# The row maxima of a second query block, moved in among the first projections of a gated two-branch attention

## Chip, core and metric

The kernel runs on one core of a Trainium2 chip. The metric is the device time of one execution in microseconds (us), over three runs the median. A difference of 0.2% is about what such a measurement can tell from none.

## What is computed

Two attention branches read the same x (2048 rows, 640 columns), each with weights of its own, 32 heads of 20 columns. A gate mixes them.

```python
def branch(x, wqkv, wo):                      # S = 2048, D = 640, H = 32, Dh = 20
    q, k, v = split_heads(x @ wqkv)           # each [H, S, Dh]
    p = softmax(q @ k.T * Dh ** -0.5)         # [H, S, S]
    return join_heads(p @ v) @ wo

g = sigmoid((x * gate_w).sum(-1, keepdims=True))
out = g * branch(x, A_wqkv, A_wo) + (1 - g) * branch(x, B_wqkv, B_wo)
```

## The kernel before

**Tiles and stages.** The 64 heads of both branches are 16 groups of four heads (`g`); two heads stand as `j` = 0, 1 in the upper and lower half of the partitions, in two `pair`s. Queries are cut into four blocks (`qb`) of 512, so there are 64 blocks, and each block's keys into eight *steps* `G` of 256: 512 steps in all (`STEPS`). In one step PE makes eight score tiles of 128 keys by 512 queries (`scores`, L639), ACT turns each into an exponential `pt` (L642), and in the next step PE multiplies these with the values into `acc` (`values`, L657).

**Row maxima.** The exponentials need each query's row maximum before they start. It is found from a second set of scores, queries by keys: `max_mm` (L565) makes a matmul (L581) for each head `j`, 128 queries (a unit `u`; eight units a block, `NS`) and 512 keys (`ch` = 0 to 3). In one way (`two`) two chunks of keys are done together: the first matmul takes the difference of the keys of two chunks (`KD`), ACT makes its relu (L585), and DVE adds the second chunk's scores and takes the largest (L589, a custom instruction with a read of its accumulator). In the other way DVE reduces one chunk directly (L592). The first block (u < 8) goes wholly in the first way; the others of group 0 only for `ch` 0 and 1. The partial maxima are in `mpart`, cleared by `max_parts` (L561) on POOL. `finish_max` (L596) reduces them (DVE), scales and splits them (POOL), and copies them on SP to a scratch `m_scr` and from there into rows of `QT` (L613, L617). Then the block is `ready`, and its score matmul yields scores less the maximum.

**Ahead of the loop.** x is turned and split into two f16 parts, and keys and queries of group 0 are projected (L937 to L943). What remains of the first projections is the generator `rest` (L951): three chunks of further query columns (`r_chunk`, 15 matmuls of 512 columns each) and 16 tiles of values (`project_v`, 15 matmuls of 161 columns each). `mms` (L375) yields after each matmul there. The loop at L959 goes over 16 *half units* of block 0: four score matmuls of maxima each (two chunks, two heads), then `go_on(BETWEEN)`, which takes products from `rest` until the planner's clock of PE has gone on by 1.3 us. Then block 0's chain (`finish_max`) is issued, and all that is left of `rest` runs at once.

**The main loop** (L1112) writes the order out by hand. A string of `STEP` (L51) lists what a step does: `e0`, `e1` a score for head 0 or 1, `m0`, `m1` a quarter of the step's maxima, `V` values, `X` a slot of projection. The maxima come from the list `maxima` (L1076), in the order of units; `next_maxima` (L1083) hands out a unit a step (eight matmuls) if the next unit is at least 14 ahead of the step, else one and a half (`RAMP`, twelve matmuls), and none if it is 15 (`LEAD`) or more ahead. At the loop's start the next unit is 8.

**Banks and queues.** Seven PSUM banks of 512 columns (`take`, `give`) hold scores, maxima and projections alike; a planner with fixed costs picks the bank that should come free first. The engines work off their own instructions in order; they wait for one another by semaphores.

Of the kernel before, what the change touches and what calls it, by code (L numbers as in the profile page):

```python
# [11 lines left out]
F32 = mybir.dt.float32  # L12
# [7 lines left out]
P = 128  # L20
# [4 lines left out]
NT = S // P  # L25
NC = D // P
# [3 lines left out]
QB = 512  # L30
NQ = S // QB
NS = 8
STEPS = 2 * NG * NQ * NS
# [19 lines left out]
        "X m0 m1 e0 m1 e0 e1 V e1 e0 m1 m0 V e1 m0 m1 m0 e0 e1 X")  # L53
LATE = "e0 e1 e0 e1 V X e0 e1 e0 e1 V"
RAMP = 1.5
BETWEEN = 1.3
NB = 7

T_SCORE, T_MODE, T_VALUES, T_READY = 0.217, 0.1, 0.85, 0.39
T_EXP, T_MAX, T_BACK = 0.478, 0.6, 0.15  # L60
REST = 6
PRODUCT = "product"
ORDER = (0, 2, 1, 3)
LOW = -3.0e38
# [4 lines left out]
def kernel(  # L69
# [10 lines left out]
    nc = tc.nc  # L80
# [42 lines left out]
    clock = {"pe": 0.0, "done": 0.0, "act": 0.0, "dve": 0.0}  # L123
    rows_free = [0.0, 0.0]
    block_end = [0.0, None]
    free_at, held = [0.0] * NB, set()
    now = [-1]

    def take():

        i = min((k for k in range(NB) if k not in held), key=lambda k: free_at[k])
        held.add(i)
        return i, banks[i]
# [16 lines left out]
    def tick_block(cost, ready=0.0):  # L150

        begin = block_end[0] if now[0] < 0 and block_end[1] == rows_free else max(rows_free) + T_MODE
        clock["pe"] = max(begin, ready)
        rows_free[:] = [clock["pe"] + cost + T_MODE] * 2
        block_end[:] = [clock["pe"] + cost, list(rows_free)]
        clock["done"] = clock["pe"] + cost + T_READY - T_MODE
# [124 lines left out]
    side = []  # L281
# [9 lines left out]
    def advance():  # L291
        for gen in list(side):
            goes = step_on(gen)
            if not goes:
                side.remove(gen)
                if goes is False:
                    parked.append(gen)
# [77 lines left out]
    def mms(i, out_ap, pairs, cost):  # L375

        if now[0] >= 0:
            tick_block(len(pairs) * cost * T_SCORE, free_at[i])
        for k, (a, b) in enumerate(pairs):
            if now[0] < 0:  # L380
                tick_block(cost * T_SCORE, free_at[i])
            nc.tensor.matmul(out_ap, a, b, start=(k == 0), stop=(k == len(pairs) - 1))  # L382
            if now[0] < 0:
                yield

    def turns(n):

# [32 lines left out]
    def run(gen):  # L420
        for _ in gen:
            pass
# [136 lines left out]
    relus, relu_at = {}, {}  # L559

    def max_parts(g, qb):  # L561
        m = mparts[g, qb] = wts.tile([P, 2, 2, 4, 4], F32, name="mpart", tag="mpart", bufs=2)
        nc.gpsimd.memset(m[:, :, 0:1 if g else 2, :, 0] if g or qb else m, LOW)

    def max_mm(u, ch, heads=(0, 1)):  # L565

        g, qb, i = unit_of(u)  # L570
        pair, t = divmod(i, 4)
        if (g, qb) not in mparts:
            max_parts(g, qb)
        q0 = qb * QB + t * P
        for j in heads:
            two = u < NS or ch < 2 and (j == 0 or g == 0)
            i, pt = take()
            ready = tick_score(j, i)
            r = slice(64 * j, 64 * j + 60)
            k = KD[g % 2 if ch == 0 else 1][r, pair] if two and ch % 2 == 0 else KT[g % 2][r, pair, ch * QB:(ch + 1) * QB]  # L580
            nc.tensor.matmul(pt, QT[g % 2][r, pair, q0:q0 + P], k, start=True, stop=True)  # L581
            m = mparts[g, qb][:, pair, j, t, ch:ch + 1]
            if two and ch % 2 == 0:
                relus[u, j] = start.tile([P, QB], F32, name="rl0", bufs=4) if u < NS else work.tile([P, QB], F32, name="rl", bufs=2)
                nc.scalar.activation(relus[u, j], pt, AF.Relu)  # L585
                back = relu_at[u, j] = spend("act", T_EXP, ready)
            elif two:
                rl = relus.pop((u, j))
                nc.vector.tensor_tensor_reduce(rl, pt, rl, 1.0, LOW, OP.add, OP.max, m)  # L589
                back = spend("dve", T_MAX, max(ready, relu_at.pop((u, j))))  # L590
            else:
                nc.vector.tensor_reduce(m, pt, axis=AX.X, op=OP.max)  # L592
                back = spend("dve", T_MAX, ready)
            give(i, back)
# [240 lines left out]
    start = start_stack.enter_context(tc.tile_pool(name="start", bufs=1))  # L835
# [44 lines left out]
            turn(j0, c)()  # L880
            yield

    max_parts(0, 0)
    load, split_next = weights_a(1)
    load()
    drains = [turn(0, c) for c in range(NC)] + [turn(4, 0)]
# [63 lines left out]
    split_next()  # L950
    rest = series(*(r_chunk(ch, (0, 1)) for ch in (1, 2, 3)), *(project_v(0, j) for j in range(0, NT, 2)))  # L951

    def go_on(us):

        end = clock["pe"] + us
        while clock["pe"] < end and next(rest, PRODUCT) is not PRODUCT:
            pass

    for half in range(2):  # L959
        for u in range(NS):  # L960
            for ch in (2 * half, 2 * half + 1):
                max_mm(u, ch, (1, 0))
            go_on(BETWEEN)
    while side:
        advance()
    chain = finish_max(0, 0)
    for _ in chain:
        go_on(0.5)
    run(rest)
    start_stack.close()  # L970

# [1 line left out]
    work = ctx.enter_context(tc.tile_pool(name="work", bufs=2))  # L973
# [99 lines left out]
        except StopIteration:  # L1073
            current.clear()

    maxima = [(u, ch) for u in range(NS, STEPS) for ch in ORDER]  # L1076
    debt = [0.0]

    def spread_of(u):
# [32 lines left out]
    for G in range(STEPS + 1):  # L1112
        g, qb, i = unit_of(G)
# [12 lines left out]
        for what in (STEP[blocks] if maxima or some else LATE + " X" * (blocks == 2)).split():  # L1126
            k = count[what] = count.get(what, 0) + 1
            if what[0] == "e":
                q = sum(count.get(f"e{j}", 0) for j in range(2)) - 1
                j = int(what[1])  # L1130
# [55 lines left out]
```

## Time and profile before

| | |
|---|---|
| median of 3 runs | 2802.12 us (2801.08 to 2802.19) |
| profiled execution, its own time | 2800.33 us |
| its span | 2798.5 us |
| mean granted clock of PE | 0.995 |
| busy: PE, ACT, DVE, POOL | 98%, 90%, 88%, 24% |

Times in the trace count from the start of the span. The half units begin at 57.6 us, the first projection of the main loop at 95.24 us, its first exponential at 97.36 us. A row of the timeline gives start, length, engine, line, operation, output <- input, and in brackets how long the engine had waited and for what. A row of the view by stretches gives the stretch, its length, then for PE, its weight loads (PEld), DVE, ACT and POOL the busy time and the number of instructions, and last PE's granted clock, the share of the DMA engines and GB/s; asked for one line alone, it has that line's engine only. A row of groups gives busy time and mean ns of one behind the bar, and then the idle time ahead of it. A matmul's length is modelled, and consecutive ones overlap.

### The profile page before, as it was taken

The page shows a single profiled execution, that of the slowest core. Times are in us where ns is not written, and L with a number is a line of the kernel's source. Part 1 is how long each engine was busy: PE and PEld are TensorE (multiplying, and loading weights), DVE is VectorE, ACT ScalarE, POOL GpSimd, SP SyncE. Part 2 cuts the span into 40 slices and gives each one's busy share as a digit, 9 for nine tenths or more (in the row PEclk, how much of TensorE's full clock was granted, in tenths as well). Part 3 has the DMA queues.
Part 4 walks back from the last instruction along what each step waited for, and adds up shares of the span by engine and source line. Part 5 has one row for each costly group of instructions (what it writes and reads, how often), then busy time and mean ns, then how long its engine had stood idle before and what let it go on. Part 6 is the DMA issues. An engine that isn't in the chain of part 4 may idle for free.

```text
span 2798.5 us, 61863 instructions
## 1 busy us (share of the span) xinstructions
PE 2744.9 (98%) x23122; PEld 939.9 (34%) x23122; DVE 2452.3 (88%) x4795; ACT 2524.6 (90%) x5106; POOL 671.9 (24%) x914
## 2 busy tenths in 40 slices
PE   6999999999999999999999999999999999999998
PEld 3433332333333332333333323333333333322222
DVE  6789899889999999888888988989988898999982
ACT  3799999999999999999999889999999999989987
POOL 5322122312222421321221212222342202200111
PEclk9999999999999999999999999999999999999999
DMA  4020102001020211202012231122201112131112
GB/s 136 19 57 14 41 11 46 7 21 25 14 64 17 62 27 54 48 8 61 21 35 70 58 77 31 38 63 54 61 23 42 33 46 63 31 88 55 42 48 75
DMA packets 172943, 124.57 MB, mean 45 GB/s; under 512 B 103264, under 2 KB 142488, under 8 KB 172640
## 3 DMA queue, kind: packets, MB, share of 16 engines
q1 hardware_dynamic: 170096, 118.99, 16.9%
q8 instruction: 181, 2.97, 0.4%
q0 software_dynamic: 1600, 0.96, 0.2%
q14 instruction: 122, 1.00, 0.1%
q10 hardware_dynamic: 944, 0.66, 0.1%
HBM read 54.54 MB, written 31.85 MB: 31 GB/s over the span
## 4 chain that ended last, share of the span: by engine, by line
PE 92%; DVE 3%; ACT 2%; DMA 1%; POOL 1%; issue 1%; SPq 0%; POOLq 0%; ACTq 0%; DVEq 0%
PE acc L657 35%; PE bank L581 19%; PE bank L382 19%; PE bank L639 18%; DVE mpart L592 2%; ACT pt L642 1%; DMA xs<-in_A_x_dram 0%; ACT rl L585 0%; DMA wv<-in_A_wqkv_dram 0%; PE bank L820 0%; DVE rl L589 0%; PE bank L190 0%; SPq L428 0%; DVE ot L743 0%; PE bank L869 0%
## 5 line engine op out<-in xcount | busy, mean ns | idle before, releaser
L642 ACT ACTIVATE pt<-bank 128x512 f32<-128x512 f32 x4096 | 2169.2, 612 | 166.7 <-PE bank L639 101.7
L592 DVE TENSOR_REDUCE mpart<-bank 128x1 f32<-128x512 f32 x2976 | 1865.2, 682 | 222.2 <-PE bank L581 114.8
L657 PE MATMUL acc<-pt,v 128*21 128x512 f32 x8192 | 1082.2, 600 | 0.6 <-DVE ot L743 0.4
L639 PE MATMUL bank<-qt,kt 64*128 64x512 f16 x4096 | 1051.7, 380 | 4.2 <-ACT pt L642 2.0
L581 PE MATMUL bank<-kt,qt 60*128 60x512 f16 x3536 | 1021.3, 380 | 5.1 <-ACT pt L642 1.7
L581 PEld LDWEIGHTS <-qt 60*128 60x128 f16 x4096 | 238.1, 94 | 862.9 <-issue 802.9
L589 DVE CUSTOM_DVE_ANT_0 rl<-bank,rl 128x512 f32<-128x512 f32 x560 | 378.7, 680 | 16.7 <-ACT rl L585 10.6
L585 ACT ACTIVATE rl<-bank 128x512 f32<-128x512 f32 x560 | 329.7, 595 | 10.7 <-PE bank L581 8.7
L639 PEld LDWEIGHTS <-kt 64*128 64x128 f16 x4096 | 235.5, 94 | 238.7 <-issue 122.8
L382 PE MATMUL bank<-xx,wbh 128*128 128x168 f16 (+3 forms) x2400 | 286.0, 239 | 2.6 <-ACT xx L873 1.9
L657 PEld LDWEIGHTS acc<-pt,v 128*21 128x21 f32 x8192 | 143.1, 99 | 428.8 <-issue 421.9
L382 PE MATMUL bank<-xx,wbl 128*128 128x168 f16 (+3 forms) x1200 | 256.1, 237 | 0.0
L751 POOL TENSOR_TENSOR ot<-ot,sq 128x512 f32<-128x512 f32 x63 | 66.0, 1047 | 773.4 <-DVE sq L748 773.4
L382 PEld LDWEIGHTS <-wbh 128*128 128x128 f16 x2400 | 189.4, 98 | 109.5 <-issue 102.0
L581 PE MATMUL bank<-kd,qt 60*128 60x512 f16 x560 | 203.8, 380 | 1.6 <-DMA kd<-dd 1.2
L382 PE MATMUL bank<-woh,o_in 128*128 128x320 f16 (+1 forms) x640 | 156.4, 302 | 5.5 <-DMA o_in<-o_scr 5.4
L411 POOL CAST cq<-fs 128x512 f16<-128x512 f32 x60 | 36.6, 610 | 521.0 <-ACT fs L409 517.4
L382 PE MATMUL bank<-wvh,xx 128*128 128x160 f16 (+1 forms) x1280 | 155.2, 234 | 0.1
L382 PEld LDWEIGHTS <-xx 128*128 128x128 f16 x1920 | 131.5, 97 | 52.3 <-issue 49.1
L382 PE MATMUL bank<-wvl,xx 128*128 128x160 f16 (+1 forms) x640 | 137.3, 231 | 0.5 <-POOL wvl L322 0.5
L382 PEld LDWEIGHTS <-wbl 128*128 128x128 f16 x1200 | 117.4, 98 | 4.3 <-issue 0.8
L382 PEld LDWEIGHTS <-o_in 128*128 128x128 f16 (+1 forms) x960 | 80.9, 97 | 97.7 <-issue 63.8
(131 smaller groups left out, 1259.1 us busy)
## 6 DMA issues: line engine op xcount, KB each, us to landing
y_scr<-y_out SPq DMA_DIRECT2D x48, 320.0 KB
y_out<-y_scr SPq DMA_DIRECT2D x32, 320.0 KB
kt<-cq SPq DMA_DIRECT2D x120, 80.0 KB
o_scr<-on SPq DMA_DIRECT2D x240, 40.0 KB
o_in<-o_scr SPq DMA_DIRECT2D x64, 96.0 KB
kt<-cq SPq DMA_DIRECT2D x136, 40.0 KB
wstage<-in_B_wqkv_dram SPq DMA_DIRECT2D x13, 400.0 KB
xs<-in_A_x_dram SPq DMA_DIRECT2D x8, 640.0 KB
```

Source lines behind the costliest of these rows:

```text
L382: nc.tensor.matmul(out_ap, a, b, start=(k == 0), stop=(k == len(pairs) - 1))
L411: nc.gpsimd.tensor_copy(hi, f)
L581: nc.tensor.matmul(pt, QT[g % 2][r, pair, q0:q0 + P], k, start=True, stop=True)
L585: nc.scalar.activation(relus[u, j], pt, AF.Relu)
L589: nc.vector.tensor_tensor_reduce(rl, pt, rl, 1.0, LOW, OP.add, OP.max, m)
L592: nc.vector.tensor_reduce(m, pt, axis=AX.X, op=OP.max)
L639: nc.tensor.matmul(et, KT[g % 2][r, pair, kt * P:(kt + 1) * P], QT[g % 2][r, pair, qb * QB:(qb + 1) * QB], start=True, stop=True)
L642: nc.scalar.activation(pt, et, AF.Exp, scale=factor(g // 4))
L657: nc.tensor.matmul(acc[32 * h:32 * h + VW, :], V[(g // 2) % 2][:, kt, (g % 2) * GH + h, :], ptiles.pop((G, kk, h)), start=(kt == 0), stop= ...
L751: nc.gpsimd.tensor_tensor(t3, t3, sq.unsqueeze(2).to_broadcast([P, 16, 32]), op=OP.mult)
```

## The change

Block 1's maxima (u = 8 to 15) are made ahead of the main loop too. There are 32 half units then, and `rest` is spread over them by count of its matmuls' columns (`streamed`, `whole`) instead of by the planner's clock: after each half unit 1/32 of it, after the last all. Block 0's chain is issued after the 16th half unit, block 1's after the last. All eight units of block 1 go by relu and difference for all four chunks. Both blocks' partial maxima are cleared at the start, whole. The main loop's list begins with unit 16, its rules are the same.

```diff
-BETWEEN = 1.3
+AHEAD = 2
...
+    streamed = [0.0]
...
                 tick_block(cost * T_SCORE, free_at[i])
+                streamed[0] += cost * T_SCORE
...
-                yield
+                yield True
...
-        nc.gpsimd.memset(m[:, :, 0:1 if g else 2, :, 0] if g or qb else m, LOW)
+        nc.gpsimd.memset(m[:, :, 0:1 if g else 2, :, 0] if g or qb >= AHEAD else m, LOW)
...
-            two = u < NS or ch < 2 and (j == 0 or g == 0)
+            two = u < AHEAD * NS or ch < 2 and (j == 0 or g == 0)
...
-    max_parts(0, 0)
+    for qb in range(AHEAD):
+        max_parts(0, qb)
...
-    def go_on(us):
+    halves_done = [0]
+    streamed[0] = 0.0
+    whole = (3 * 3 * NC + NT * 3 * NC * 0.33) * T_SCORE
+
+    def go_on(share):
...
-        end = clock["pe"] + us
-        while clock["pe"] < end and next(rest, PRODUCT) is not PRODUCT:
+        while streamed[0] < share * whole and next(rest, None) is not None:
             pass
...
-    for half in range(2):
-        for u in range(NS):
-            for ch in (2 * half, 2 * half + 1):
-                max_mm(u, ch, (1, 0))
-            go_on(BETWEEN)
-    while side:
-        advance()
-    chain = finish_max(0, 0)
-    for _ in chain:
-        go_on(0.5)
+    for block in range(AHEAD):
+        for half in range(2):
+            for u in range(block * NS, (block + 1) * NS):
+                for ch in (2 * half, 2 * half + 1):
+                    max_mm(u, ch, (1, 0))
+                halves_done[0] += 1
+                go_on(halves_done[0] / (2 * AHEAD * NS))
+        while side:
+            advance()
+        run(finish_max(0, block))
     run(rest)
...
-    maxima = [(u, ch) for u in range(NS, STEPS) for ch in ORDER]
+    maxima = [(u, ch) for u in range(AHEAD * NS, STEPS) for ch in ORDER]
```

On ACT, at the end of the part ahead of the loop, before: `rl` is a relu for maxima, two of them make a half unit, and `v` with `gates` drains a tile of values.

```order
L585 ACTIVATE rl_856<-bank_94 128x512
L585 ACTIVATE rl_859<-bank_89 128x512
L537 ACTIVATE v_86<-bank_92 128x8x20
L542 ACTIVATE gates<-bank_92,inv_g 128x1
L537 ACTIVATE v_86<-bank_93 128x8x20
L542 ACTIVATE gates<-bank_93,inv_g 128x1
L537 ACTIVATE v_86<-bank_91 128x8x20
L542 ACTIVATE gates<-bank_91,inv_g 128x1
```

The same place on ACT in the changed kernel:

```order
L587 ACTIVATE rl_1080<-bank_90 128x512
L587 ACTIVATE rl_1083<-bank_94 128x512
L587 ACTIVATE rl_1101<-bank_92 128x512
L587 ACTIVATE rl_1104<-bank_95 128x512
L539 ACTIVATE v_86<-bank_91 128x8x20
L544 ACTIVATE gates<-bank_91,inv_g 128x1
L587 ACTIVATE rl_1125<-bank_89 128x512
L587 ACTIVATE rl_1128<-bank_92 128x512
```

Before, nine tiles of values are drained one after the other behind the last relus; in the changed kernel relus go on to the end, with a tile of values behind each pair or each second pair.

On ACT at the start of the main loop, before: `fs` drains a projection, `pt` is an exponential, `rl` a relu for block 1's maxima.

```order
L409 ACTIVATE fs<-bank_91 128x176
L628 TENSOR_LOAD esc_103
L642 ACTIVATE pt<-bank_94 128x512
L585 ACTIVATE rl<-bank_89 128x512
L585 ACTIVATE rl<-bank_95 128x512
L642 ACTIVATE pt<-bank_92 128x512
L642 ACTIVATE pt<-bank_90 128x512
L642 ACTIVATE pt<-bank_95 128x512
L642 ACTIVATE pt<-bank_93 128x512
L642 ACTIVATE pt<-bank_90 128x512
L585 ACTIVATE rl<-bank_91 128x512
```

The same place on ACT in the changed kernel:

```order
L411 ACTIVATE fs<-bank_90 128x176
L630 TENSOR_LOAD esc_103
L644 ACTIVATE pt<-bank_93 128x512
L644 ACTIVATE pt<-bank_91 128x512
L644 ACTIVATE pt<-bank_94 128x512
L644 ACTIVATE pt<-bank_89 128x512
L644 ACTIVATE pt<-bank_95 128x512
L644 ACTIVATE pt<-bank_92 128x512
L644 ACTIVATE pt<-bank_90 128x512
L644 ACTIVATE pt<-bank_93 128x512
L411 ACTIVATE fs<-bank_91 128x168
```

The relus are gone from steps 0 and 1; in step 2 they are back, two a step.

On SP, behind the copies of group 0's queries, before: `m_scr` and `qt<-m_scr` are a block's chain, `wstage` the weights of the next values, `kd` and `kt` the keys of group 1.

```order
L613 DMA m_scr_123<-m4r 16x4x32 x4
L617 DMA qt_80<-m_scr_123 4x512 x4
L240 DMA wstage<-in_A_wqkv_dram 128x5x160
L428 DMA kd_85<-dd 40x1x512
L430 DMA kd_85<-dd 20x512
L613 DMA m_scr_124<-m4r 16x4x32 x4
```

The same place on SP in the changed kernel:

```order
L615 DMA m_scr_123<-m4r 16x4x32 x4
L619 DMA qt_80<-m_scr_123 4x512 x4
L615 DMA m_scr_124<-m4r 16x4x32 x4
L619 DMA qt_80<-m_scr_124 4x512 x4
L241 DMA wstage<-in_A_wqkv_dram 128x5x160
L430 DMA kd_85<-dd 40x1x512
```

Block 1's chain stood among the copies of group 1's keys and now stands ahead of the weights for the next values.

More of the change, by code (lines that the diff above doesn't have):

```diff
@@ L583, in max_mm @@
             if two and ch % 2 == 0:
[L584 removed]
+                relus[u, j] = start.tile([P, QB], F32, name="rl0", bufs=4) if u < AHEAD * NS else work.tile([P, QB], F32, name="rl", bufs=2)
                 nc.scalar.activation(relus[u, j], pt, AF.Relu)
```

## The prediction

> **What bounds the kernel now.** I read the page first: the busy times, then the chain that ended last.
>
> ```profile
> span 2798.5 us, 61863 instructions
> PE 2744.9 (98%) x23122; PEld 939.9 (34%) x23122; DVE 2452.3 (88%) x4795; ACT 2524.6 (90%) x5106; POOL 671.9 (24%) x914
> PE 92%; DVE 3%; ACT 2%; DMA 1%; POOL 1%; issue 1%; SPq 0%; POOLq 0%; ACTq 0%; DVEq 0%
> ```
>
> TensorE (PE) is busy for 98% of the span and carries 92% of the chain. No later idle time can swallow what is won or lost at the front, so the sum can be made at the front alone. The program order says how far the front goes: apart from the numbers of PSUM banks, every engine's instructions stand in the old order again from about step 17 of the 512 steps of the main loop.
>
> Next I cut the front of the main loop into stretches of eight steps. One step has eight exponentials (L642), so 64 of them mark a stretch; the second view gives all engines in the same stretches, and in steps 15 to 17 alone (24 exponentials).
>
> ```profile
> 97.30:152.80 55.50, 34.35 (x64) 0.97 0.08 18
> 152.80:200.10 47.30, 34.11 (x64) 1.00 0.31 72
> 283.10:324.50 41.40, 33.97 (x64) 1.00 0.29 61
> ```
> ```profile
> 97.30:152.80 55.50, 52.64 (x397) 19.34 (x394) 47.47 (x114) 47.42 (x96) 14.34 (x16) 0.97 0.08 18
> 152.80:200.10 47.30, 46.39 (x394) 16.66 (x393) 41.09 (x88) 43.87 (x92) 11.84 (x17) 1.00 0.31 72
> 195.20:210.75 15.55, 15.46 (x143) 5.36 (x140) 13.60 (x30) 15.28 (x33) 1.10 (x2) 1.00 0.22 59
> ```
>
> The first eight steps take 55.5 us, the next eight 47.3, ordinary ones 41.4. In the order of before, steps 0 to 9 carry 12 score matmuls for maxima each (eight are the even rate), since the lead of the maxima is still being built up. In the first stretch PE, ScalarE (ACT) and VectorE (DVE) all have idle time (52.6, 47.4 and 47.5 of 55.5): it isn't one full engine but twelve maxima fighting eight exponentials for seven banks. In steps 15 to 17, with the even rate and two relus a step, ACT is busy for 15.28 of 15.55 us.
>
> Ahead of the loop lie the first projections with block 0's maxima among them (the stretch from 57.60), and from 86.15 a tail of products alone.
>
> ```profile
> 57.60:95.24 37.64, 37.07 (x348) 22.46 (x349) 24.23 (x78) 25.23 (x67) 28.22 (x45) 1.00 0.20 44
> 86.15:95.24 9.09, 9.09 (x130) 9.06 (x129) 1.90 (x8) 4.55 (x18) 0.89 (x4) 1.00 0.03 4
> ```
>
> PE is full there (37.07 of 37.64), ACT (25.23) and DVE (24.23) are not. So a maximum that is moved ahead pays full PE time there, and frees the loop of work that three engines contend for.
>
> **The change part by part.** *(a) 16 more half units ahead of the loop.* A half unit is four score matmuls of maxima and the products behind it. These are PE's rows for two, with six products of 512 columns between, and the first score matmuls of two more, with 15 value products between:
>
> ```profile
> 59.67 0.39 PE L581 MATMUL bank<-kd,qt 60*128 60x512 f16 x2
> 60.20 1.04 PE L382 MATMUL bank<-xx,wbh 128*128 128x512 f16 x4
> 61.08 0.59 PE L382 MATMUL bank<-xx,wbl 128*128 128x512 f16 x2
> 61.60 0.39 PE L581 MATMUL bank<-kd,qt 60*128 60x512 f16 x2
> 64.08 1.47 PE L382 MATMUL bank<-xx,wbh 128*128 128x512 f16 x6
> 82.24 0.39 PE L581 MATMUL bank<-kd,qt 60*128 60x512 f16 x2
> 83.94 0.39 PE L581 MATMUL bank<-kd,qt 60*128 60x512 f16 x2
> ```
>
> Six products cost six times (1.47 − 0.38)/5 = 0.218 us, or 1.31; a half unit without its products is 61.60 − 59.67 − 1.31 = 0.62 us. From the value products: 83.94 − 82.24 = 1.70, less 15 × 9.09/129 = 1.06, leaves 0.64. I take 0.64. 16 × 0.64 = **+10.2 us**. The products themselves (45 × 0.218 + 240 × 0.0705 = 26.7 us) only move: 26.7 + 16 × 0.64 + a wait of 0.5 = 37.4 gives the measured 37.6 within 0.2. The new half unit lasts about 0.64 + 26.7/32 = 1.47 us.
>
> *(b) Waits in this part.*
>
> ```profile
> 73.28 0.23 PE L382 MATMUL bank<-wvl,xx 128*128 128x161 f16 x1 [0.55 <-POOL wvl L322]
> 57.62 0.50 PE L581 MATMUL bank<-kd,qt 60*128 60x512 f16 x2 [1.16 <-DMA kd<-dd]
> 53.62 3.19 SPq L428 DMA_DIRECT2D kd<-dd  x4
> 66.59 3.19 SPq L428 DMA_DIRECT2D kd<-dd  x4
> ```
>
> The wait for wvl goes (−0.5): value products begin after 45 of the first ones, at four a half unit some 12 half units in, near 75 us, and POOL released the first at 73.28. Another comes late instead: the ninth half unit reads the second key differences. For the first ones the third copy began at 53.62 + 1.6 = 55.2 and PE was released at 57.62, 2.4 later; for the second it begins at 68.2, so they are there at 70.6. The ninth half unit now stands at 57.6 + 8 × 0.64 + 32 × 0.218 = 69.7: **+0.9**. Then the banks. These are the two relus and the two maxima of one half unit whose first score starts at 59.67:
>
> ```profile
> 60.09 1.09 ACT L585 ACTIVATE rl<-bank 128x512 f32<-128x512 f32 x2 [0.97 <-PE bank L581]
> 60.72 0.69 DVE L589 CUSTOM_DVE_ANT_0 rl<-bank,rl 128x512 f32<-128x512 f32 x1 [0.64 <-ACT rl L585]
> 61.34 0.69 DVE L589 CUSTOM_DVE_ANT_0 rl<-bank,rl 128x512 f32<-128x512 f32 x1
> 61.95 0.08 DVE L589 DVE_READ_ACCUMULATOR2_ANT mpart<- 128x1 f32 x1
> ```
>
> Its banks come free 1.0, 1.5, 1.7 and 2.4 us after its start. The next but one pair of scores wants banks at 1.47 + 0.22 = 1.7, with one or two of seven held by products: just enough, or late by 0.1 to 0.2 where a product changes its bank. The engines' own loads fit: DVE 24.23 + 16 × 1.23 = 44 and ACT 25.23 + 16 × 1.0 = 41 of some 47 us. Ends: 0 and 32 × 0.12 = 4 us; I take **+1.0**, near the rows in which no half unit waits for a bank. Part (a) and (b): +10.2 − 0.5 + 0.9 + 1.0 = **+11.6**; the loop starts near 107 instead of 95.2.
>
> *(c) The first 16 steps of the loop.* They hold 176 score matmuls of maxima before and 112 after: none in steps 0 and 1, eight in each of 2 to 15, with two relus a step, as in steps 15 to 17 of before. ACT's groups in those three steps:
>
> ```profile
> L642 ACT ACTIVATE pt<-bank 128x512 f32<-128x512 f32 x24 | 12.8, 680 | 0.3 <-PE bank L639 0.3
> L585 ACT ACTIVATE rl<-bank 128x512 f32<-128x512 f32 x6 | 3.4, 643 | 0.0
> L409 ACT ACTIVATE fs<-bank 128x128 f32<-128x128 f32 x3 | 1.1, 379 | 0.0
> ```
>
> Neighbours overlap: the groups add up to 17.3 us in 15.28 of busy ACT, so each counts 0.88 of its time: 0.47 an exponential, 0.50 a relu, 0.32 a drain of a projection. Steps 0 and 1: 8 × 0.47 + 0.32 = 4.1 us each. Steps 2 to 15: not below 8 × 0.47 + 2 × 0.50 + 0.32 = 5.1; not above the 47.30/8 = 5.9 of the second stretch, which still carried ten maxima a step. I take the row with the same mix, 15.55/3 = 5.18. Sum 2 × 4.1 + 14 × 5.18 = 80.7 against 55.5 + 47.3 = 102.8: **−22.1** (ends −23.4 and −12).
>
> *(d) The clock.* PE's granted clock (the third figure from the end) by single microseconds at the loop's start:
>
> ```profile
> 98.00:99.00 1.00, 0.78 (x4) 0.20 (x4) 0.09 (x1) 1.00 (x3) 0.00 (x0) 1.00 0.89 281
> 99.00:100.00 1.00, 0.88 (x4) 0.30 (x4) 0.94 (x3) 1.00 (x3) 0.00 (x0) 1.00 0.00 0
> 100.00:101.00 1.00, 0.92 (x5) 0.25 (x4) 1.00 (x4) 1.00 (x3) 0.00 (x0) 0.70 0.00 0
> 101.00:102.00 1.00, 1.00 (x5) 0.22 (x3) 1.00 (x2) 1.00 (x3) 0.00 (x0) 0.50 0.00 0
> 102.00:103.00 1.00, 1.00 (x7) 0.63 (x6) 1.00 (x3) 1.00 (x3) 0.00 (x0) 0.50 0.00 0
> 103.00:104.00 1.00, 1.00 (x10) 1.00 (x9) 0.37 (x1) 0.34 (x1) 0.00 (x0) 0.59 0.00 0
> ```
>
> It fell to half for about 3.4 us (0.6 + 1 + 1 + 0.8) after thinly filled ones, a loss of up to 1.7 us that is part of the 102.8. Steps 0 and 1 are thinner on PE after the change (step 0 has one projection and eight scores in 4.1 us), so I expect the dip again, partly beside ACT's own queue: **+1.0** (0 to +3.4).
>
> The Trainium skill, "TensorE: Matmul & The Clock Gate", Part 1, has the gate fall to half only after a whole idle window of about 3.4 us. By that rule the dip before could not be, since PE was 0.78 and 0.88 busy; the length of the dip agrees with its window, its cause doesn't. By the rule alone (d) would be −1.7 instead of +1.0.
>
> *(e) What else moves.* Block 0's chain to its copies had the tail of products as cover (86 to 95 us); now block 1's 16 half units cover it, some 23 us, and block 1's chain has until step 8. On SP the copy of the next value weights stands behind block 1's chain: before, it was issued at 95.97, 8.0 us after the last maximum at 87.93; now that is some 9 us into the loop, 12 with its landing, and DVE first reads it in step 3, about 18 us in. Were that cover gone, DVE would wait those few us with full banks behind it. The larger memset of POOL runs ahead of the first products, where POOL's queue is short: nothing.
>
> ```profile
> 95.97 0.41 SPq L240 DMA_DIRECT2D wstage<-in_A_wqkv_dram  x1
> 87.93 0.09 DVE L589 DVE_READ_ACCUMULATOR2_ANT mpart<- 128x1 f32 x1
> ```
>
> Sum: +11.6 − 22.1 + 1.0 = **−9.5 us**. The profiled execution took 2800.3, so it becomes 2790.8; the median of the runs shown, 2802.1, stands 1.8 above it. I say 2792.0, the rounded middle of 2790.8 and 2792.6.
>
> **The rivals.** *Everything is covered*: no bank waits, no dip, steps at ACT's 5.1. −0.5 + 10.2 + 0.9 − 23.4 − 1.7 = −14.5: 2786 to 2788. The skill's rule on the clock would help this one by 2.7; chance 0.10. *The loop stays crowded*: what slows its first steps isn't only the extra maxima, and steps 2 to 15 take 5.9. The gain is 12, and +11.6 + 1.0 eats it: 2800 to 2803, no change. For it speaks that no engine was full in the first stretch; against it, that steps 15 to 17 are 5.18 at the even rate; 0.14. *The banks run out ahead of the loop*, the one that is slower: if a half unit can only start when the last one's banks are free, it takes 2.4 us instead of 1.47, 32 × 0.9 = +29, and the time is near 2820. Over half units of (22.1 − 1.0 − 0.9 + 37.4)/32 = 1.80 us the change loses. Against it: 1.70 us, with a whole value tile inside, passes without a wait for a bank; 0.05. That the maxima aren't moved is excluded by the order.
>
> **How the numbers follow.** My forecast, 2788 to 2798, has 0.71. A range of 2786 to 2799 leaves out most of the crowded loop, the slower rival and little else, under 2 in 10. 0.2%, about what a measurement can tell from no change, is 5.6 us: faster means under 2796.5. That is the covered case and nearly all of the forecast, 0.79; the crowded loop and the forecast's end make 0.15 for no change; 0.06 for slower.
>
> **What would show it.** The stretch from 57.6 to the loop's first projection at 48 to 50 us (47 if no bank waits; over 58 and the slower rival is right); a wait of PE for the second key differences of about 1 us; the first 64 exponentials within 38 to 41 us and the next 64 within 40 to 43; a clock below 1 near the loop's start. The prediction is wrong if steps 2 to 15 stay over 5.5 us, or if the gain of the front is given back behind step 17.

## The result, and the profile after

The changed kernel takes 2794.29 us (median of nine runs, 2792.92 to 2795.49), the kernel before 2801.97 (nine runs, 2801.08 to 2802.19). The ratio is 0.9973, with a 95% interval of 0.9964 to 0.9981: faster by 7.7 us. The forecast was 2792.0, with a range of 2786 to 2799. The profiled execution took 2794.76 us, 5.6 less than the one of before; the spans differ by 5.5 (2798.5 and 2793.0), and that 5.5 is accounted for below. Lines of the changed kernel stand two higher than those of before: the score of a maximum is L583, the relu L587, the exponential's score L641, the exponential L644.

The page of the changed kernel, its busy times and its chain:

```profile
span 2793.0 us, 61900 instructions
PE 2742.3 (98%) x23122; PEld 937.4 (34%) x23122; DVE 2443.7 (87%) x4795; ACT 2531.5 (91%) x5122; POOL 673.2 (24%) x914
PE 93%; DVE 3%; ACT 1%; DMA 1%; SPq 0%; issue 0%; POOL 0%; POOLq 0%; ACTq 0%; DVEq 0%
```

PE stays the engine of the chain, with as many matmuls as before (23122); ACT has 16 instructions more, the new relus. The page's averages show no more than that: the change is in the first 200 us. Next the view by stretches, first from the first half unit to the loop's first projection, then steps 0 and 1, then steps 2 to 15:

```profile
58.40:108.88 50.48, 49.67 (x414) 24.71 (x415) 43.91 (x139) 41.89 (x99) 28.18 (x44) 1.00 0.15 34
...
110.80:118.85 8.05, 7.46 (x63) 3.08 (x60) 0.00 (x0) 8.00 (x18) 0.53 (x2) 1.00 0.24 56
118.85:193.90 75.05, 74.78 (x663) 27.72 (x663) 59.96 (x135) 73.50 (x156) 25.48 (x30) 1.00 0.23 53
```

And the exponentials alone, 64 in a stretch, as before:

```profile
110.80:152.20 41.40, 33.59 (x64) 1.00 0.10 24
152.20:193.90 41.70, 33.16 (x64) 1.00 0.36 82
```

The part ahead of the loop went from 37.64 to 50.48 us. The first two stretches of the loop went from 55.50 and 47.30 to 41.40 and 41.70: the dear front of the loop is gone, and both now cost what an ordinary stretch of before did (41.40). In steps 0 and 1 DVE does nothing at all and ACT is full (8.00 of 8.05); in steps 2 to 15 PE (74.78 of 75.05) and ACT (73.50) are both nearly full, while DVE has slack (59.96).

From step 16 on, each stretch of eight steps takes as long as before, within 0.08 us (two neighbours differ by 0.18 and −0.18), but for one. In steps 288 to 295, PE waits for the attention's output on its way through the scratch, and then runs at half clock. The changed kernel's waits of PE between 1610 and 1659 us:

```profile
PE bank L384 <- DMA o_in<-o_scr: 5.5, 1, 5.5
```

The kernel before waits there too, for 5.4 us, but its stretch takes 47.92 us and that of the changed kernel 48.65. Behind the wait, the changed kernel in stretches of 2 us (the granted clock is the third figure from the end):

```profile
1650.00:1652.00 2.00, 1.83 (x8) 0.68 (x10) 0.00 (x0) 0.00 (x0) 0.00 (x0) 0.50 0.77 211
1652.00:1654.00 2.00, 2.00 (x10) 0.34 (x12) 1.37 (x3) 1.40 (x3) 0.00 (x0) 0.50 0.34 75
1654.00:1656.00 2.00, 2.00 (x14) 0.23 (x6) 1.28 (x3) 0.45 (x2) 0.00 (x0) 0.64 0.49 177
```

And the kernel before:

```profile
1654.00:1656.00 2.00, 0.00 (x0) 0.00 (x0) 0.00 (x0) 0.00 (x0) 0.00 (x0) 0.50 0.42 92
1656.00:1658.00 2.00, 1.68 (x6) 0.63 (x6) 0.00 (x0) 0.00 (x0) 0.00 (x0) 0.50 0.71 211
1658.00:1660.00 2.00, 2.00 (x11) 0.45 (x14) 1.46 (x3) 1.26 (x3) 0.00 (x0) 0.50 0.32 71
1660.00:1662.00 2.00, 2.00 (x18) 0.35 (x14) 1.65 (x4) 1.03 (x3) 0.00 (x0) 0.93 0.52 184
```

Both have 6.8 us of half clock, but before 2.8 of it passed while PE still stood, and 4.0 fell on work (1.68 + 2 + 0.28); in the changed kernel 5.3 fell on work (1.83 + 2 + 1.44). Half of the difference of 1.3 is the 0.7. It is a matter of where the wait lies in the clock's pieces of time, not of the change; the last section comes back to it. The whole difference of the spans:

| part | before | after | difference |
|---|---|---|---|
| up to the first half unit | 57.62 | 58.43 | +0.8 |
| first half unit to first exponential | 39.74 | 52.42 | +12.7 |
| 128 exponentials, steps 0 to 15 | 102.80 | 83.09 | −19.7 |
| the stretch of steps 288 to 295 | 47.92 | 48.65 | +0.7 |
| all else | | | 0.0 |
| span | 2798.5 | 2793.0 | −5.5 |

The +0.8 is not the change's either: the code up to there differs in one memset, and PE's half clock at the start lasted 13.65 us in this execution and 10.24 in that of before, four and three pieces of 3.41 us. e7, e9 and e10 below have that memset too, but 10.24 us of half clock, and their first half unit stands at 57.22 to 57.61. The medians differ by 2.2 us more than the spans, because the profiled execution of before lies 1.6 under its median and this one 0.5 over.

### The profile page after: what moved, and what is told of

The parts are those of the page before. It is cut to its first block, busy times and chain, and to the rows that moved or that the text cites. A ratio compares the mean times of both kernels' runs of the same rounds, so it can differ in the third digit from the quotient of the medians.

```text
span 2793.0 us, 61900 instructions
## 1 busy us (share of the span) xinstructions
PE 2742.3 (98%) x23122; PEld 937.4 (34%) x23122; DVE 2443.7 (87%) x4795; ACT 2531.5 (91%) x5122; POOL 673.2 (24%) x914
## 3 DMA queue, kind: packets, MB, share of 16 engines
q8 instruction: 181, 2.97, 0.4%
## 4 chain that ended last, share of the span: by engine, by line
PE 93%; DVE 3%; ACT 1%; DMA 1%; SPq 0%; issue 0%; POOL 0%; POOLq 0%; ACTq 0%; DVEq 0%
PE acc L659 35%; PE bank L384 20%; PE bank L583 19%; PE bank L641 18%; DVE mpart L594 2%; ACT pt L644 1%; DMA xs<-in_A_x_dram 0%; PE bank L822 0%; DMA wv<-in_A_wqkv_dram 0%; PE bank L191 0%; PE bank L871 0%; DVE rl L591 0%; SPq L430 0%; DMA kd<-dd 0%; DVE ot L745 0%
## 5 line engine op out<-in xcount | busy, mean ns | idle before, releaser
L644 ACT ACTIVATE pt<-bank 128x512 f32<-128x512 f32 x4096 | 2167.4, 613 | 162.1 <-PE bank L641 97.7
L594 DVE TENSOR_REDUCE mpart<-bank 128x1 f32<-128x512 f32 x2944 | 1842.7, 681 | 230.8 <-PE bank L583 120.5
L641 PE MATMUL bank<-qt,kt 64*128 64x512 f16 x4096 | 1046.7, 380 | 3.2 <-DVE mpart L594 1.5
L583 PE MATMUL bank<-kt,qt 60*128 60x512 f16 x3520 | 1015.6, 380 | 4.0 <-ACT pt L644 1.3
L583 PEld LDWEIGHTS <-qt 60*128 60x128 f16 x4096 | 236.5, 94 | 860.2 <-issue 798.6
L591 DVE CUSTOM_DVE_ANT_0 rl<-bank,rl 128x512 f32<-128x512 f32 x576 | 386.8, 677 | 9.9 <-ACT rl L587 5.7
L587 ACT ACTIVATE rl<-bank 128x512 f32<-128x512 f32 x576 | 336.7, 594 | 9.1 <-PE bank L583 8.5
L641 PEld LDWEIGHTS <-kt 64*128 64x128 f16 x4096 | 234.4, 94 | 237.7 <-issue 123.3
L583 PE MATMUL bank<-kd,qt 60*128 60x512 f16 x576 | 204.4, 380 | 2.0 <-DMA kd<-dd 1.8
```

Of the source, the lines that this page charges most:

```text
L641: nc.tensor.matmul(et, KT[g % 2][r, pair, kt * P:(kt + 1) * P], QT[g % 2][r, pair, qb * QB:(qb + 1) * QB], start=True, stop=True)
L644: nc.scalar.activation(pt, et, AF.Exp, scale=factor(g // 4))
```

## The experiments

The theory to be tested, A, is that of the prediction: what a maximum costs depends on where it stands. In the crowded first steps it takes the time of three engines, ahead of the loop only PE's 0.16 us a matmul (0.64/4) plus waits for banks, and what was given up as cover is paid besides. The rival B is named in each expectation. Ratios are taken against the kernel before, measured again beside each, and the profiled spans are cut as in the table above. "Front" is the time from the first half unit to the first exponential; the last column has the first 64 exponentials and the next 64, steps 0 to 7 and 8 to 15.

| kernel | median us | ratio (95%) | front | 64 + 64 exponentials |
|---|---|---|---|---|
| before | 2801.97 | 1 | 39.74 | 55.48 + 47.32 |
| after | 2794.29 | 0.9973 (0.9964 to 0.9981) | 52.42 | 41.40 + 41.69 |
| e1, spread alone | 2809.25 | 1.0027 (1.0017 to 1.0037) | 47.16 | 55.71 + 47.32 |
| e2, old pace | 2799.07 | 0.9993 (0.9984 to 1.0003) | 57.16 | 41.41 + 41.71 |
| e3, mixed ways | 2800.61 | 0.9996 (0.9987 to 1.0006) | 58.21 | 41.41 + 41.69 |
| e4, three blocks | 2804.39 | 1.0010 (1.0001 to 1.0020) | 71.29 | 34.27 + 39.83 |
| e5, steeper ramp | 2801.97 | 1.0000 (0.9991 to 1.0010) | 39.77 | 62.14 + 41.63 |
| e6, lead 12 | 2810.91 | 1.0034 (1.0022 to 1.0046) | 39.77 | 53.29 + 42.37 |
| e12, relus in the loop | 2804.52 | 1.0009 (1.0000 to 1.0019) | 39.76 | 58.69 + 47.32 |
| e8, pairs | 2802.34 | 0.9999 (0.9990 to 1.0009) | 60.02 | 41.40 + 41.68 |
| e7, more products early | 2793.77 | 0.9972 (0.9961 to 0.9982) | 51.65 | 41.40 + 41.69 |
| e9, an eighth bank | 2791.84 | 0.9965 (0.9952 to 0.9978) | 50.63 | 41.40 + 41.68 |
| e10, e7 and e9 | 2791.84 | 0.9963 (0.9950 to 0.9977) | 49.32 | 41.40 + 41.69 |
| e11, lead 17 | 2803.64 | 1.0005 (0.9995 to 1.0014) | 52.68 | 43.48 + 41.68 |

### The parts of the change, one at a time

**e1_spread_only**: the products are spread evenly, but only block 0's maxima stand among them.

```diff
-AHEAD = 2
+AHEAD = 1
```

> The changed kernel with block 0 alone ahead of the loop (16 half units), the products still spread evenly over them. Theory A (the gain is block 1's maxima taken out of the crowded first steps; the spreading gives nothing by itself): no tail of products is left to cover block 0's chain, about 10 us from its last maximum to its rows in QT, so the loop's first exponential comes near 105 instead of 97.4, its first 128 exponentials take about 100 us as before, and the time is near 2810. Rival B (the even spreading is what gained): 2798 or less.

It took 2809.25 us, 7.3 more than before, as A had it. The loop's front is as dear as before (55.71 and 47.32), and the part ahead of it grew by 7.4. The waits of PE in e1 between 95 and 107 us:

```profile
PE bank L641 <- DMA qt<-m_scr: 4.8, 1, 4.8
```

The first scores of the loop wait for block 0's maxima on their way back to QT. In the kernel before, the tail of products covered that way; spread evenly, the products are used up with the last maximum. So the even spread alone is a loss; in the change, block 1's half units have become the cover. The wait is 4.8 of the 7.4: PE also waits 1.9 us for wvl (0.5 before), since the value products start earlier, and it runs at half clock for the 3.4 us from 74.6 on. From the last maximum to the first score it is 5.9 us (99.02 to 104.96), where I had expected about 10. That the time came out as expected is in part luck.

**e2_old_pace**: both blocks ahead, but each half unit followed by 1.3 us of products, as before.

```diff
-                go_on(halves_done[0] / (2 * AHEAD * NS))
+                go_on(min(1.0, halves_done[0] * 1.3 / whole))
```

> The changed kernel with the products handed out at the old pace, 1.3 us a half unit, so that they are used up after some 20 of the 32 half units and the last 11 run bare. Theory A (a half unit is 0.64 us of PE unless DVE's 1.23 us binds it): 20.6 x 1.94 + 11.4 x 1.25 = 54 us ahead of the loop instead of 50.4, less the waits for banks and key differences (about 2), so 2796 to 2798. Rival B (PE's work is the same, the pace does not matter): 2794.

2799.07 us: the loop gains as in the change, and the front loses 4.7 of it (57.16 against 52.42). A's direction, 1.1 over its range. At that pace the products run out, and the last half units stand alone. Windows of e2 there:

```profile
96.50:100.00 3.50, 3.38 (x29) 1.60 (x27) 2.62 (x9) 3.31 (x10) 0.00 (x0) 1.00 0.04 8
100.00:103.50 3.50, 3.29 (x14) 1.11 (x13) 3.50 (x11) 3.50 (x8) 0.00 (x0) 1.00 0.00 0
103.50:106.90 3.40, 3.08 (x12) 0.53 (x11) 3.40 (x13) 3.21 (x7) 0.00 (x0) 0.50 0.00 0
106.90:110.30 3.40, 3.10 (x11) 0.61 (x11) 3.40 (x13) 2.87 (x6) 0.00 (x0) 0.50 0.00 0
```

Without products DVE is full in every window from 100.00 on, and a half unit lasts 0.98 to 1.30 us instead of 0.64. PE fell to half clock from 103.50 for 10.2 us. Its records show it busy before that (3.29 of 3.50), but a matmul's length is modelled, and these are 14 scores; the last section counts them.

**e3_mixed**: block 1's second two chunks are reduced directly, as before the change.

```diff
-            two = u < AHEAD * NS or ch < 2 and (j == 0 or g == 0)
+            two = u < NS or ch < 2 and (j == 0 or g == 0)
```

> The changed kernel with block 1's chunks 2 and 3 reduced directly by DVE, as they were before, instead of by relu and difference. Theory A: eight half units ahead of the loop then hold four reductions of 0.6 us each, DVE needs 2.4 us instead of 1.23 and binds, +0.95 x 8 = +7.5, so 2801 to 2802. Rival B (PE bounds that part whatever the form): 2794.

2800.61 us, 0.4 under A's numbers. The front takes 58.21, 5.8 more than in the change. The stretch of e3 with those half units:

```profile
85.00:105.00 20.00, 19.14 (x177) 10.79 (x177) 18.39 (x47) 10.98 (x32) 1.17 (x4) 1.00 0.02 3
```

DVE is busy for 18.39 of 20.00 us and ACT for 10.98: a half unit then takes DVE four reductions instead of two, and lasts 2.25 to 2.6 us. So the way by relu and difference is needed for the gain ahead of the loop, since there ACT has room.

### Where a maximum is cheap

**e4_three**: a third block goes ahead of the loop.

```diff
-AHEAD = 2
+AHEAD = 3
...
-        m = mparts[g, qb] = wts.tile([P, 2, 2, 4, 4], F32, name="mpart", tag="mpart", bufs=2)
+        m = mparts[g, qb] = wts.tile([P, 2, 2, 4, 4], F32, name="mpart", tag="mpart", bufs=3)
```

> The changed kernel with a third block's maxima ahead of the loop (48 half units, 0.56 us of products each; three buffers of partial maxima). Theory A (only the crowded steps were dear; a unit in an even step costs 1.2 us, ahead of the loop at least 2 x 0.64): +16 half units at 1.3 us or more by DVE, less the products that they share, about +13, a longer wait for the second key differences, +2, and eight more steps without maxima, -8 x 1.25 = -10: 2797 to 2801. Rival B (every block that is moved ahead gains as much as block 1 did): 2786.

2804.39 us, slower than before; A's direction, but 3 us above its numbers. The front grows by 18.9 against the change (71.29), the loop's first 16 steps get 9.0 shorter (74.10 against 83.09). That B's 2786 was far off shows that more is not better: 64 matmuls leave even steps at 9.0/64 = 0.14 us each, and cost 18.9/64 = 0.30 each ahead. In the change, the same count left crowded steps at 19.7/64 = 0.31 and cost 12.7/64 = 0.20. A window of e4:

```profile
110.00:120.00 10.00, 10.00 (x86) 4.80 (x86) 9.11 (x29) 8.28 (x21) 0.00 (x0) 1.00 0.01 3
```

DVE is at 9.11 of 10.00 and ACT at 8.28. With 26.7/48 = 0.56 us of products each, half units should last 1.20; they alternate between 1.21 and 1.68, and the 0.47 lies at the third and fourth score, which need nothing but a free bank there. That is what A had priced too low.

**e5_ramp2**: the kernel before, whose loop builds up its lead with two units a step instead of one and a half.

```diff
-RAMP = 1.5
+RAMP = 2.0
```

> The kernel before with RAMP = 2: sixteen score matmuls of maxima a step for seven steps instead of twelve for ten and more. Theory A (at twelve a step relus and sums fall into alternate steps, so that ACT binds one step and DVE the next; at sixteen each step is alike): seven steps of about 7.4 us by DVE (12 x 0.61) and nine of 5.25 make 99 us for the first 128 exponentials instead of 102.8, time 2798. Rival B (each maximum over the even rate costs the same 0.4 us): 2802. Rival C (seven banks cannot hold more maxima, steps over 8.4 us): 2808 or more.

2801.97 us: A's 2798 was wrong, B's 2802 right. The two stretches of e5, of 64 exponentials each, and 10 us in the midst of the first:

```profile
97.80:159.90 62.10, 57.94 (x413) 20.83 (x411) 54.54 (x130) 49.60 (x100) 14.41 (x16) 0.95 0.08 18
159.90:201.50 41.60, 41.60 (x378) 15.31 (x376) 34.16 (x72) 41.44 (x89) 11.90 (x17) 1.00 0.34 79
...
125.00:135.00 10.00, 9.29 (x68) 2.88 (x61) 9.86 (x23) 6.99 (x15) 0.84 (x3) 1.00 0.02 2
```

The crowd only moves: 62.14 and 41.63 make 103.8 against 102.8. At 16 maxima a step DVE is the bound (9.86 of 10.00), and each of the first five steps takes 8.1 to 9.0 us. A steeper dose within the loop does not escape the price of the crowd.

**e6_lead12**: the kernel before with a shorter lead, so that fewer extra maxima are to be made at the front.

```diff
-LEAD = 15
+LEAD = 12
```

> The kernel before with LEAD = 12: the lead is built up from 8 to 11 only. Theory A (the catching up is what makes the first steps long): six or seven crowded steps fewer, about -8; the last 12 instead of 15 steps run without maxima, +3 x 1.2 = +3.6; time near 2797. Rival B (the first 16 steps are long for another reason): the second stretch of 64 exponentials stays near 47 us, time 2802 to 2805.

2810.91 us, 14 above A's numbers. Front and end were as A had them: the first 128 exponentials take 7.1 us less (53.29 and 42.37), the last 16 steps 3.8 more. The two stretches of e6:

```profile
98.30:151.55 53.25, 50.08 (x387) 18.99 (x385) 43.60 (x104) 45.94 (x94) 15.24 (x18) 0.97 0.07 18
151.55:193.95 42.40, 42.17 (x382) 15.54 (x378) 34.73 (x73) 41.67 (x88) 11.03 (x16) 1.00 0.36 79
```

But the profiled span is 7.3 longer, since 7.2 were lost in steps 320 to 327 and 2.4 in steps 192 to 199 (−7.1 + 3.8 + 7.2 + 2.4 = 6.3; the start of this execution has most of the rest). The waits of PE in e6 in the first of these:

```profile
PE bank L639 <- DMA qt<-m_scr: 6.8, 1, 6.8
```

With a lead of 12 a block's maxima are not back in QT when its first score wants them. There are three such waits, 10.2 us in all; one of 2.4 is the loss of steps 192 to 199. This execution is the shortest of the six, 3.2 under their median, and what the others lose besides isn't seen. So the crowd at the front is the price of a lead that the middle needs.

**e12_relus_in_loop**: the kernel before, with block 1 in the loop by relu and difference for all chunks. The relus are told apart by chunk pair, and there are four of them.

```diff
-            two = u < NS or ch < 2 and (j == 0 or g == 0)
+            two = u < 2 * NS or ch < 2 and (j == 0 or g == 0)
...
-        nc.gpsimd.memset(m[:, :, 0:1 if g else 2, :, 0] if g or qb else m, LOW)
+        nc.gpsimd.memset(m[:, :, 0:1 if g else 2, :, 0] if g or qb >= 2 else m, LOW)
```

> The kernel before, block 1's maxima still in the loop but all four chunks by relu and difference (four buffers for relus, whole memset of the partial maxima). DVE has 16 instructions of 0.61 us less in steps 0 to 5, ACT 16 relus of 0.48 us more. Theory A (DVE is what the crowded steps wait for): the first 64 exponentials take 48 to 51 us instead of 55.5, time 2795 to 2798. Rival B (ACT is as much in the way as DVE, so that only moving the work ahead helps): 55 to 60 us, time 2802 or more.

2804.52 us, 2.5 more than before: B was right. Most of the first stretch of e12 (57.60 of 58.69 us), and 10 us of it:

```profile
97.40:155.00 57.60, 55.16 (x386) 19.77 (x383) 37.20 (x111) 53.63 (x111) 14.38 (x16) 0.94 0.06 16
...
110.00:120.00 10.00, 9.96 (x79) 4.05 (x76) 5.15 (x16) 9.92 (x22) 1.77 (x2) 1.00 0.00 1
```

DVE falls to 37.20 us, and ACT goes to 53.63 of 57.60 (9.92 of 10.00 in the window): in those steps ACT's time is as dear as DVE's. The half clock lasts 6.8 us there instead of 3.4, which is worth 1.7 us at most, so that the stretch stays above the 55.5 of before without it. What the loop gained in the change came by the other place of the maxima, not by their other way.

### The terms ahead of the loop

**e8_pairs**: the change, with the products in portions of double size after every second half unit.

```diff
-                go_on(halves_done[0] / (2 * AHEAD * NS))
+                if halves_done[0] % 2 == 0:
+                    go_on(halves_done[0] / (2 * AHEAD * NS))
```

> The changed kernel with products after every second half unit only: eight score matmuls in a row, 16 changes between scores and products fewer. Theory A (0.2 us of a half unit's 0.64 is the change, but the seventh and eighth score have to wait for banks, about 0.4 us each time): 2795 to 2798. Rival B (the change alone counts, 16 x 0.2): 2791.

2802.34 us; A's direction, but its size (2795 to 2798) is wrong. PE's first scores of a pair of half units in e8, and of the next pair:

```profile
102.14 0.39 PE L583 MATMUL bank<-kd,qt 60*128 60x512 f16 x2
...
102.58 0.38 PE L583 MATMUL bank<-kd,qt 60*128 60x512 f16 x2
103.21 0.86 PE L583 MATMUL bank<-kt,qt 60*128 60x512 f16 x2 [0.25 <-ACT rl L587]
...
105.80 0.39 PE L583 MATMUL bank<-kd,qt 60*128 60x512 f16 x2
```

This pair, with 24 value products, lasts 105.80 − 102.14 = 3.66 us; 2 × 0.64 + 24 × 0.0705 is 2.97. The first half unit takes 0.44, 0.2 less than 0.64, as both theories had it; the second, with the products, takes 3.22, and that is 0.89 more than 0.64 + 24 × 0.0705. The last two scores of the pair stand for banks: eight scores want eight, there are seven. A had put that at 0.4 a pair. The order of four scores and a few products is what lets seven banks suffice.

**e7_front**: the change, with 1.3 portions of products in the first eight half units.

```diff
-                go_on(halves_done[0] / (2 * AHEAD * NS))
+                go_on((halves_done[0] + 0.3 * min(halves_done[0], NS)) / (2 * AHEAD * NS + 0.3 * NS))
```

> The changed kernel with the first eight half units given 1.3 shares of the products, so that the ninth comes after the second key differences have landed. Theory A: the wait of 0.7 us for them goes, and some of the bank waits in the first eight half units (0.6): 2793.0 to 2793.5. Rival B (the wait turns into waits for banks further on, with fewer products there): 2794.3.

2793.77 us, 0.5 under the change, which the time alone cannot tell apart. In its profile the wait for the second key differences is gone, and the front is 0.8 shorter: that term is what the prediction said it was.

**e9_eight_banks**: the change, with the accumulator lent as an eighth bank until the loop begins, and cleared again there.

```diff
-    banks = [psum.tile([P, QB], F32, name=f"bank{i}") for i in range(NB)]
+    banks = [psum.tile([P, QB], F32, name=f"bank{i}") for i in range(NB)] + [acc]
...
-    i = min((k for k in range(NB) if k not in held), key=lambda k: free_at[k])
+    i = min((k for k in range(nb[0]) if k not in held), key=lambda k: free_at[k])
...
     run(rest)
+    nb[0] = NB
+    nc.vector.memset(acc, 0.0)
```

> The changed kernel with the accumulator's bank lent to scores and products until the loop starts (eight banks instead of seven), and cleared once more before the loop. Theory A (what a half unit takes over 0.64 us and its products, apart from the key differences, is waiting for a bank: 2.4 us in all): that goes, the time from the first half unit to the first exponential falls from 52.4 to about 50, less a few tenths for the clearing; 2792. Rival B (those waits are for the relu or for DVE, not for a bank): 52.4 stays, 2794.3.

2791.84 us, 2.4 under the change, as A had it (2792). The part from the first half unit to the first exponential in e9:

```profile
57.60:108.20 50.60, 49.75 (x435) 25.70 (x436) 45.50 (x145) 42.57 (x102) 28.48 (x45) 1.00 0.15 34
```

The front takes 50.63 instead of 52.42, and every half unit in the value part now takes 1.42 or 1.49 us, the bare sum. So the waits for banks were 1.8 us of the front at least.

**e10_front_eight**: e7 and e9 together.

> The eight banks of the run before and the fuller first half units together. Theory A: both waits go, 52.4 - 2.4 - 0.7 = 49.3 us to the first exponential, time 2791.2 to 2791.7. Rival B (only the key differences' wait goes): 2793.7.

The front came to 49.32, the 49.3 that was expected, 1.3 under e9's. Yet the time is e9's, 2791.84. The waits of PE in e10 between 1605 and 1656 us:

```profile
PE bank L385 <- DMA o_in<-o_scr: 6.3, 2, 5.6
```

These are 6.3 us in two waits, the longer of them 5.6; the half clock behind it lasts 10.2 us instead of 6.8, three pieces instead of two, and 6.4 of it fall on work instead of 5.3. That stretch takes 1.4 us more than in the change, two later ones together 0.6. What this execution won at the front it gave back there. e9 and e10 are the fastest kernels of this study; their intervals overlap the change's.

**e11_lead17**: the change, with a longer lead.

```diff
-LEAD = 15
+LEAD = 17
```

> The changed kernel with LEAD = 17: steps 0 and 1 have maxima too, the lead is 16 throughout and the last 17 steps run without maxima. Theory A (in an even step a unit of maxima costs about 1.2 us wherever it stands): first 64 exponentials +2.4, last sixteen steps -2.4, time 2794. Rival B (a longer lead takes waits out of the middle of the loop, as the shorter one put 9 us in): 2791 or less.

2803.64 us: 9.4 more than the change, which no theory had. The first stretch grew by 2.1 (2.4 expected), but the last 16 steps gave back 0.8 only (2.4 expected), and between steps 64 and 495 the profile has 11.4 us more, scattered over many stretches (2.6 in steps 288 to 295, 2.1 and 1.8 in the two stretches from step 256, 1.6 in steps 448 to 455). The waits of PE in e11:

```profile
PE bank L384 <- DMA o_in<-o_scr: 11.2, 4, 8.1
```

In the changed kernel it is one such wait of 5.5 us. That explains some 6 of the 11.4. This profiled execution was itself 4 us above its kernel's median, so part of the rest may be chance; what else the lead disturbs stays open.

## Why the prediction was right, point by point

**(a) The half units.** Forecast 0.64 us each without products, and right: in the changed kernel a half unit with four products of 512 columns takes 1.51 us (0.64 + 4 × 0.218), and many with value products have no excess either. PE's first scores of half units near the end, and two at the start:

```profile
60.08 0.39 PE L583 MATMUL bank<-kd,qt 60*128 60x512 f16 x2
61.59 0.39 PE L583 MATMUL bank<-kd,qt 60*128 60x512 f16 x2
...
71.79 0.50 PE L583 MATMUL bank<-kd,qt 60*128 60x512 f16 x2 [0.63 <-DMA kd<-dd]
...
96.48 0.39 PE L583 MATMUL bank<-kd,qt 60*128 60x512 f16 x2
...
98.23 0.39 PE L583 MATMUL bank<-kd,qt 60*128 60x512 f16 x2
...
99.72 0.39 PE L583 MATMUL bank<-kd,qt 60*128 60x512 f16 x2
```

99.72 − 98.23 = 1.49 is the bare sum with 12 value products; 98.23 − 96.48 = 1.75 has a wait for banks of 0.26 in it.

**(b) The waits.** The one for wvl is gone. The ninth half unit waits for the second key differences (the row at 71.79): 0.63 us, against a forecast of 0.9. The banks were mis-sized: forecast +1.0, measured 2.4 over the 32 half units, within the bound of 4. I took a value near the rows without a wait; the row of the four banks (free 1.0 to 2.4 us after the start, wanted after 1.7) was the one to follow. e9 shows the cause: with an eighth bank 1.8 of them go. Sum of (a) and (b): +12.7 against +11.6.

**(c) The loop.** Forecast −22.1, or −21.1 with the clock; measured −19.7. Steps 0 and 1 took 8.05 (forecast 8.2). Steps 2 to 15 took 75.05, or 5.36 each, against 5.18 forecast. 1.9 of these 2.5 us fall in steps 4 to 6 (5.79, 6.15 and 5.50). What stands on DVE near there:

```profile
126.77 0.98 DVE L235 TENSOR_REDUCE m<-wstage 128x1 f32<-128x800 f32 x1
...
133.93 0.27 DVE L178 TENSOR_REDUCE e<-bank 1x1 f32<-1x128 f32 x1
...
134.76 0.32 DVE L184 TENSOR_SCALAR dg<-ident,e 1x1 f32<-1x1 f32 x2
...
140.71 0.47 DVE L216 COPY wrow<-both 32x1 f32<-32x1 f32 x3
```

These find the scales of the next weights, by a chain of small instructions between PE, DVE and the others. Steps 15 to 17, from which I took the 5.18, have none of it: that row had the same count of scores, but not the same small work. The same chain stands again far behind the front, in steps 315 and 316:

```profile
1761.82 0.94 DVE L235 TENSOR_REDUCE m<-wstage 128x1 f32<-128x800 f32 x1
...
1768.64 0.27 DVE L178 TENSOR_REDUCE e<-bank 1x1 f32<-1x128 f32 x1
```

There, in both kernels, steps 316 and 317 take 5.8 and 6.2 us, and the steps on either side of them 5.1 to 5.2. So the cost goes with these instructions; that they are its cause is still read from their places, and no run took them away. The rival of a crowded loop (5.9 a step) is dead, in the profile and by e5 and e12: what made those steps dear was the number of maxima in them.

**(d) The clock.** Forecast +1.0; the dip didn't come back. The first two pieces of 3.40 us of the changed loop:

```profile
110.80:114.20 3.40, 2.93 (x29) 1.37 (x25) 0.00 (x0) 3.35 (x7) 0.53 (x2) 1.00 0.06 7
114.20:117.60 3.40, 3.40 (x33) 1.41 (x29) 0.00 (x0) 3.40 (x9) 0.00 (x0) 1.00 0.18 27
```

29 and 33 matmuls in 3.4 us kept the clock at 1.00; I had called these steps thin by ACT's pace, though the projection's matmuls fill them. So this term measured 0. The −1.7 by the rule of the Trainium skill, "TensorE: Matmul & The Clock Gate", Part 1, was a wrong sum of mine: the 102.8 of before holds the old dip and the 80.7 holds none, so a loop without a dip is (c) alone, and the −1.7, in the covered rival too, counted the old dip twice. The rule itself agrees with these two rows, but it isn't the full account: in e2 half clock came behind a window that was not idle, with 14 scores in 3.50 us. Further down, the same Part tells also of a kernel whose clock swung because PE stood often and briefly between groups of matmuls; I had gone by its table of the two states alone. That the +1.0 was wrong was luck for the number: without it the forecast would have been 1.0 us further off.

**(e) What else moves.** No wait for the value weights, no cover lost: e1 shows what stood at stake (4.8 us of PE's wait). That no later idle time swallows what is won at the front held too: behind step 16 nothing changed but the 0.7 of steps 288 to 295, and that stretch depends on the clock's pieces, not on the front.

The terms of the miss, in terms of the profile: −9.5 forecast, −5.5 measured, with +1.1 ahead of the loop, +1.4 in it, +0.8 at the start and +0.7 in steps 288 to 295. The first two are the prediction's misses, the last two belong to these executions. Against the medians the forecast was 2.3 us low. Of the signs that I had named, two lie just outside their bounds (50.48 us up to the loop's first projection against 48 to 50, 41.40 for the first 64 exponentials against 38 to 41), the second 64 lie within, and the clock below 1 didn't come.

## What to carry to other kernels

Price a piece of work where it leaves and where it goes: here a maximum's matmul cost 0.31 us among crowded steps, 0.14 among even ones, and 0.20 to 0.30 among products, so that the second block paid for its move and the third did not. When work is packed closer, count the banks that are held at the new period, and look for what the old gap covered. A difference of 1 us between two single executions can lie in the clock alone, so account for it place by place before it is put down to an edit.

## What the runs showed of the hardware

PE's half clock comes in pieces of 3.41 us: 10.2 or 13.7 us at the start of an execution, 6.8 or 10.2 behind the wait in steps 288 to 295 (3.4 in e6, where that wait is shorter). The Trainium skill, "TensorE: Matmul & The Clock Gate", Part 1, calls this window free-running, and the runs agree: in the kernel before half clock begins at 100.41 and at 1653.47 us, 455 pieces apart, and the same wait costs more or less by where it falls. With the wait and the half clock that falls on work, the stretch of steps 288 to 295 adds up in kernel after kernel (us):

| kernel | stretch | wait | half clock on work | stretch − wait − half of that |
|---|---|---|---|---|
| e5 | 47.94 | 5.64 | 3.51 | 40.5 |
| before | 47.92 | 5.39 | 3.98 | 40.5 |
| e7 | 48.41 | 5.54 | 4.68 | 40.5 |
| after | 48.65 | 5.53 | 5.28 | 40.5 |
| e2 | 49.19 | 5.66 | 6.10 | 40.5 |
| e10 (two waits) | 50.09 | 6.31 | 6.44 | 40.6 |

The other kernels give 40.5 to 40.6 as well, but for e6 (40.7) and e11 (40.8).

The half clock also comes without a standstill in the records: in the piece of e2 that begins at 100.12 us PE is busy for 3.20 of 3.41 us, and half clock follows. But these are 12 scores, and four scores start within 0.44 us where nothing holds them up (e8), so they are 1.3 us of work, a share of 0.38. I counted so in all fourteen traces: 0.109 us for a score (two start together, one in each half of the rows, and the next two 0.22 us later), 0.218 for a product of 512 columns (others in proportion), 0.125 for a matmul with the values. Of some 11,200 pieces at full clock, half clock followed the 34 whose share was 0.407 or less, and none of those with 0.410 or more. The dip of the kernel before follows a share of 0.29, with PE busy for 2.58 us in the records; a piece of e1 with PE busy for only 1.62 us, but 19 matmuls and a share of 0.41, kept the clock. So what sorts the pieces is the work that PE streams in them, not its busy time. This is a count over these traces, in which a few records can be missing; no run set the share on purpose.
